# A delta-rule attention and a low-rank mixer in one kernel: two small products retiled, the square root table moved, a new order of all steps

## The chip, the cores and the metric

The kernel runs on one core of a Trainium2 chip. A core has five engines, each with its own in-order list of instructions: TensorE (PE, matmuls; its weight loads are listed as PEld), VectorE (DVE), ScalarE (ACT), GpSimd (POOL) and SyncE (SP, which here only issues DMA transfers). SP, POOL and ACT each own queues to the DMA engines. [...] TensorE reads its operands from SBUF and writes to PSUM, which holds 8 banks here, used as four pairs.

The metric is the device time of one execution in microseconds (us). A profile is one execution taken by the hardware profiler; it gives the span from the first to the last instruction and the execution's own time around it.

## What is computed

Two blocks follow one another (batch B=4, heads H=8, sequence S=768, head size D=48, model width 384, rank 32, hidden width 1536), all in fp32:

```python
# block 1: a delta-rule recurrence for each batch and head
k_n = k / (norm(k) + 1e-6)
for t in range(S):
    y[t]  = q[t] @ state
    v_old = k_n[t] @ state
    state = state + beta[t] * outer(k_n[t], v[t] - v_old)
# x: (B, S, 384), the heads side by side
# block 2: a mixer of low rank over the tokens, then a two-layer net over the channels
h = (x.transpose(0, 2, 1) @ U) @ V       # U: 768 x 32, V: 32 x 768
u = x + h.transpose(0, 2, 1)
out = u + relu(u @ w_ch1) @ w_ch2        # 384 -> 1536 -> 384
```

## The kernel before

**Units and chunks.** The recurrence is worked in chunks of 64 tokens. A unit n (0 to 7) is half a batch: 6 chunks of all 8 heads; batch b has the units 2b and 2b+1. For each unit there are, in this order: transfers of k, q, v and a shifted copy of k (`load`, line 524, issued by SP, POOL and, for unit 0, half of the keys by ACT); turning k and q to have the head size on the partitions (`turn`, TensorE transposes, line 639, in runs of six; the copy out of PSUM is `placed`, lines 648 to 653); products of the turned keys with keys and queries (`products`, line 666); the norms (`norms`, line 586: a square root on ScalarE, then VectorE from line 589); the inversion of a triangular matrix for each chunk and head. The inversion is a substitution on VectorE (`blocks`: transposed in at line 742, then the pairs of lines 751 and 757, transposed out at line 764), followed by small matmuls that join blocks (`joins`, lines 808, 822, 848 to 869, and copies by ScalarE, lines 813, 856, 875, 887). `prepare` (lines 971 and 982) makes from these the operands of the recurrence. VectorE does the substitutions of two units one after the other, since both use the same buffers.

**Recurrence.** `recur(b)` goes through the batch's 12 chunks, one after another. In each there is a product with the old state (line 1020), a subtraction on VectorE (line 1033), an update of the state (line 1048 on TensorE, 1059 on VectorE) and the outputs (lines 931 and 945, copied to X by ScalarE at line 915).

**Mixer.** `front(b, i)` handles 256 tokens (i = 0, 1, 2) of batch b. For i = 0 it first makes U^T x for the whole batch (line 1338), with PSUM's 128 partitions cut into four groups of 32, one for each column group of the array. Before the change, group g adds up the three blocks of 128 tokens with c = g mod 2: the groups 0 and 2 hold the sum over the even blocks, 1 and 3 the sum over the odd ones, each twice. VectorE copies it to `tt` (line 1344). V lies in `v_sb` four times below itself, so that 64 rows of V against 64 rows of `tt` add the two partial sums. The product with V (line 1357) is made of four matmuls, each on its own 64x64 quarter of the array: two halves of the output rows for each of two blocks of 128 tokens; VectorE adds it to X (line 1362), TensorE turns the sum (line 1381), ScalarE copies it to `ut` (line 1384).

**Channel net.** `wide(b, i)` does the first layer (`channels`, line 1442, relu at line 1407) and the second (`narrow`, line 1562) with a scheme that needs seven block products in place of eight; for the last batch the first layer too has such a scheme (`quick`, line 1241). Sums into X are at line 1482, the stores at lines 1488 and 1494.

**Weights.** U, V, w_ch1 and w_ch2 (slices 0 to 13) come as 64-bit numbers and are converted to fp32: a transfer (`start`, line 1131), a scaling on ScalarE (`raised`, line 1143), three steps on VectorE (lines 1157, 1164, 1171). Their three landing buffers are used in turn.

**Modes of the array.** A matmul whose operands use all 128 rows and columns takes the whole array. Smaller ones are put on tiles of it: 64x64 (lines 555, 666, 808, 822, 931 to 1048, 1357), 32x32 (848 to 869) or 128x32 (1338).

**What sets the order.** Every step is a `yield` of a Python generator. A text in the kernel (`ORDER`, lines 144 to 344) gives for each generator the positions of its steps in one list of 2139; `run` works it off in that order. An engine's list is its share of these steps in order. The costs given to `op(...)` and the conditions given to `need(...)` and `emitted(...)` served the search of that list; they put no wait into the program. The waits come from the data alone.

**Square root.** [...] The table with the square root is loaded by an instruction that the compiler puts ahead of the first operation that needs it. The kernel has an operation meant to bring that about early (line 535, a square root of one column `warm`), which in the order before stands at position 750, after the first norms.

Of the kernel before, what the change touches and what calls it, by code (L numbers as in the profile page):

```python
# [8 lines left out]
FP32 = mybir.dt.float32  # L9
# [7 lines left out]
L = 64  # L17
# [10 lines left out]
def kernel(  # L28
# [69 lines left out]
    def act(n):  # L98
        return 0.16 + n / 1200.0
# [45 lines left out]
    add_up b0 i0 f00: 658 659 660; add_up b0 i0 f03: 623 625 647; add_up b0 i1 f00: 774 778 789; add_up b0 i1 f03:  # L145
    794 808 809; add_up b0 i2 f00: 902 910 928; add_up b0 i2 f03: 978 981 985; add_up b1 i0 f00: 1073 1111 1134;
    add_up b1 i0 f03: 1122 1125 1132; add_up b1 i1 f00: 1253 1269 1279; add_up b1 i1 f03: 1276 1278 1292; add_up b1
    i2 f00: 1417 1426 1442; add_up b1 i2 f03: 1475 1481 1485; add_up b2 i0 f00: 1583 1621 1630; add_up b2 i0 f03:
    1643 1645 1653; add_up b2 i1 f00: 1724 1726 1731; add_up b2 i1 f03: 1797 1799 1801; add_up b2 i2 f00: 1872 1886
    1915; add_up b2 i2 f03: 1924 1925 1932; add_up b3 i0 f00: 2051 2052 2053; add_up b3 i0 f03: 2067 2068 2070;  # L150
    add_up b3 i1 f00: 2089 2090 2091; add_up b3 i1 f03: 2095 2096 2097; add_up b3 i2 f00: 2111 2112 2113; add_up b3
    i2 f03: 2105 2108 2109; blocks n0: 49 75 79 80 81 82 83 84 85 86 88 94 98 99 110 111 117 120; blocks n1: 126 142
    148 155 169 180 184 187 189 191 200 209 211 213 219 224 225 229; blocks n2: 478 498 502 503 506 511 514 517 518
    520 525 533 534 539 540 541 547 550; blocks n3: 686 699 708 710 719 720 725 727 733 736 738 740 743 744 747 748
    751 754 760 761 762 763 764 772 781 784 785 806 811 823 824 825 827 831; blocks n4: 947 959 970 971 979 986 987
    990 994 996 997 1000 1001 1016 1024 1029 1030 1033 1037 1043 1046 1047 1048 1051 1052 1053 1056 1057 1058 1062
    1065 1069 1071 1079; blocks n5: 1102 1139 1141 1143 1144 1153 1161 1163 1169 1176 1177 1178 1179 1190 1201 1209
    1211 1213 1215 1219 1221 1224 1227 1229 1235 1240 1248 1249 1252 1254 1257 1259 1262 1264; blocks n6: 1429 1451
    1452 1453 1457 1464 1471 1478 1490 1496 1499 1505 1507 1510 1514 1516 1526 1528 1535 1536 1537 1545 1546 1547
    1552 1553 1556 1558 1560 1562 1563 1565 1568 1573; blocks n7: 1595 1609 1614 1618 1632 1635 1648 1658 1661 1662  # L160
    1670 1674 1676 1681 1684 1687 1691 1693 1699 1700 1705 1711 1712 1714 1715 1718 1719 1722 1725 1729 1733 1738
    1739 1762; both f0: 2034; both f1: 2000; both f2: 1992; both f3: 2063; both f4: 1986; both f5: 2047; channels b0
    i0 e0: 522 524; channels b0 i0 e1: 535 546; channels b0 i0 e2: 549 558; channels b0 i0 e3: 561 581; channels b0
    i0 e4: 583 603; channels b0 i0 e5: 606 609; channels b0 i1 e0: 753 755; channels b0 i1 e1: 757 758; channels b0
    i1 e2: 765 766; channels b0 i1 e3: 767 769; channels b0 i1 e4: 770 771; channels b0 i1 e5: 777 786; channels b0
    i2 e0: 861 872; channels b0 i2 e1: 876 887; channels b0 i2 e2: 891 899; channels b0 i2 e3: 904 918; channels b0
    i2 e4: 925 940; channels b0 i2 e5: 942 968; channels b1 i0 e0: 1049 1059; channels b1 i0 e1: 1060 1064; channels
    b1 i0 e2: 1066 1067; channels b1 i0 e3: 1074 1080; channels b1 i0 e4: 1082 1084; channels b1 i0 e5: 1085 1108;
    channels b1 i1 e0: 1214 1217; channels b1 i1 e1: 1228 1230; channels b1 i1 e2: 1231 1232; channels b1 i1 e3: 1241
    1266; channels b1 i1 e4: 1267 1270; channels b1 i1 e5: 1272 1273; channels b1 i2 e0: 1369 1377; channels b1 i2  # L170
    e1: 1385 1387; channels b1 i2 e2: 1394 1408; channels b1 i2 e3: 1410 1427; channels b1 i2 e4: 1435 1444; channels
    b1 i2 e5: 1450 1469; channels b2 i0 e0: 1548 1569; channels b2 i0 e1: 1570 1577; channels b2 i0 e2: 1578 1579;
    channels b2 i0 e3: 1581 1594; channels b2 i0 e4: 1597 1600; channels b2 i0 e5: 1602 1603; channels b2 i1 e0: 1695
    1696; channels b2 i1 e1: 1698 1704; channels b2 i1 e2: 1710 1713; channels b2 i1 e3: 1728 1734; channels b2 i1
    e4: 1743 1744; channels b2 i1 e5: 1754 1785; channels b2 i2 e0: 1843 1846; channels b2 i2 e1: 1855 1856; channels
    b2 i2 e2: 1857 1861; channels b2 i2 e3: 1871 1883; channels b2 i2 e4: 1895 1902; channels b2 i2 e5: 1910 1921;
    copies f0: 2014 2018; copies f1: 1964 1987; copies f2: 1969 1974; copies f3: 2038 2040; copies f4: 1968 1971;
    copies f5: 2016 2036; cut f0 k0 to0: 2030; cut f0 k0 to1: 2035; cut f0 k1 to1: 2069; cut f1 k0 to0: 1990; cut f1
    k0 to1: 2079; cut f1 k1 to1: 2002; cut f2 k0 to0: 2050; cut f2 k0 to1: 2006; cut f2 k1 to1: 2004; cut f3 k0 to0:
    2049; cut f3 k0 to1: 2077; cut f3 k1 to1: 2062; cut f4 k0 to0: 2059; cut f4 k0 to1: 2007; cut f4 k1 to1: 2026;  # L180
    cut f5 k0 to0: 2056; cut f5 k0 to1: 2093; cut f5 k1 to1: 2057; diagonals n0 h0: 192 202 204 208 218 221;
    diagonals n0 h1: 164 178 183 188 198 207; diagonals n1 h0: 305 306 312 313 319 337; diagonals n1 h1: 262 265 276
    280 334 340; diagonals n2 h0: 585 592 594 613 637 648; diagonals n2 h1: 608 610 611 614 620 621; diagonals n3 h0:
    836 839 844 848 867 880; diagonals n3 h1: 843 845 879 886 888 890; diagonals n4 h0: 1088 1091 1092 1103 1124
    1136; diagonals n4 h1: 1093 1106 1107 1116 1130 1148; diagonals n5 h0: 1274 1280 1290 1315 1332 1337; diagonals
    n5 h1: 1308 1314 1340 1345 1348 1370; diagonals n6 h0: 1607 1626 1627 1629 1631 1636; diagonals n6 h1: 1587 1588
    1589 1601 1616 1617; diagonals n7 h0: 1765 1766 1767 1768 1812 1813; diagonals n7 h1: 1769 1773 1780 1787 1818
    1839; first f0: 2029; first f1: 1989; first f2: 1979; first f3: 2048; first f4: 2015; first f5: 2031; front b0
    i0: 485 501 504 508 510 512; front b0 i1: 523 532 548 551; front b0 i2: 644 653 654 664; front b1 i0: 1003 1013
    1023 1025 1036 1041; front b1 i1: 1075 1094 1152 1157; front b1 i2: 1301 1324 1334 1342; front b2 i0: 1506 1512  # L190
    1515 1529 1532 1533; front b2 i1: 1561 1574 1598 1610; front b2 i2: 1659 1660 1666 1669; front b3 i0: 1919 1920
    1926 1927 1931 1933; front b3 i1: 1936 1940 1945 1948; front b3 i2: 1949 1950 1954 1955; gather b0 i0 h0 c0
    finalFalse: 650; gather b0 i0 h0 c0 finalTrue: 638; gather b0 i0 h0 c1 finalTrue: 730 1181; gather b0 i0 h1 c0
    finalFalse: 693; gather b0 i0 h1 c0 finalTrue: 711 737; gather b0 i0 h1 c1 finalFalse: 695; gather b0 i0 h1 c1
    finalTrue: 716; gather b0 i1 h0 c0 finalFalse: 807; gather b0 i1 h0 c0 finalTrue: 814; gather b0 i1 h0 c1
    finalTrue: 856 1244; gather b0 i1 h1 c0 finalFalse: 819; gather b0 i1 h1 c0 finalTrue: 858 1220; gather b0 i1 h1
    c1 finalFalse: 829; gather b0 i1 h1 c1 finalTrue: 846; gather b0 i2 h0 c0 finalFalse: 973; gather b0 i2 h0 c0
    finalTrue: 983; gather b0 i2 h0 c1 finalTrue: 1045 1097; gather b0 i2 h1 c0 finalFalse: 998; gather b0 i2 h1 c0
    finalTrue: 1050 1192; gather b0 i2 h1 c1 finalFalse: 999; gather b0 i2 h1 c1 finalTrue: 1027; gather b1 i0 h0 c0
    finalFalse: 1126; gather b1 i0 h0 c0 finalTrue: 1147; gather b1 i0 h0 c1 finalTrue: 1204 1305; gather b1 i0 h1 c0  # L200
    finalFalse: 1166; gather b1 i0 h1 c0 finalTrue: 1202 1304; gather b1 i0 h1 c1 finalFalse: 1175; gather b1 i0 h1
    c1 finalTrue: 1182; gather b1 i1 h0 c0 finalFalse: 1283; gather b1 i1 h0 c0 finalTrue: 1296; gather b1 i1 h0 c1
# [140 lines left out]
    1841 1922 1929 1938 1941 1944 1951  # L343
    """
    ORDER = [x.rsplit(":", 1) for x in " ".join(ORDER.split()).split("; ")]
    ORDER = {int(y): name for name, at in ORDER for y in at.split()}

    def name_of(part):

# [1291 lines left out]
```

## Time and profile before

| | us |
|---|---|
| median of three runs | 614.36 |
| the three runs | 611.83, 614.36, 616.7 |
| the profiled execution, its own time | 617.97 |
| its span | 616.3 |
| TensorE busy in the span | 581.1 |
| VectorE busy | 393.1 |
| ScalarE busy | 232.4 |
| POOL busy | 96.5 |
| U^T x, line 1338, 96 records | 8.8 busy, 0.498 each |
| V product, line 1357, 96 records | 10.8 busy, 0.523 each |
| the one load of the square root table, at line 586 | 1.283 |

Times on the page are measured from the span's start. The time of one instruction is from its issue to its end; matmuls overlap, so a matmul's time is longer than its share of the engine, and the share is read from the distance of two starts. An fp32 matmul appears as two records. The row PEclk on the page is the clock granted to TensorE, in tenths of full speed, for each of 40 equal slices of the span. The chain of waits follows the last instruction back to what released it, step by step; a time on it is a time that the end had to wait for.

### The profile page before, as it was taken

How to read it: one execution, taken by the hardware profiler on the slowest of the kernel's cores; microseconds unless marked ns; L12 is line 12 of the kernel's file. 1: busy time of each engine (PE TensorE's matmuls, PEld its weight loads, DVE VectorE, ACT ScalarE, POOL GpSimd, SP SyncE). 2: the span in 40 equal slices, each digit the busy share in tenths (PEclk: the TensorE clock that was granted, in tenths of full speed). 3: DMA queues.
4: the chain of work that ended last, by engine and by line, in shares of the span. 5: the costliest groups of instructions: out<-in, count | busy, mean ns of one | idle time of the engine just before them, and what ended most of it. 6: DMA issues, size and time to landing. Idle time of an engine off the chain costs nothing.

```text
span 616.3 us, 23450 instructions
## 1 busy us (share of the span) xinstructions
PE 581.1 (94%) x10548; PEld 499.2 (81%) x10548; DVE 393.1 (64%) x971; ACT 232.4 (38%) x463; POOL 96.5 (16%) x169
## 2 busy tenths in 40 slices
PE   5598986899999999999999999999999999999997
PEld 4487875678888988888988988888989877655997
DVE  5878684688689616989697248998774124224352
ACT  2655754436512354126423452255152331234100
POOL 7141130401202501203101403013001000000000
PEclk9955555789999999999999999999999999999999
DMA  9924369512011510300122302211010000100010
GB/s 145 180 52 115 106 191 188 111 30 71 22 30 29 83 34 17 70 26 23 30 87 46 69 3 65 57 24 33 14 45 12 29 4 1 38 0 1 1 50 29
DMA packets 63845, 33.28 MB, mean 54 GB/s; under 512 B 50816, under 2 KB 61824, under 8 KB 63744
## 3 DMA queue, kind: packets, MB, share of 16 engines
q1 hardware_dynamic: 56800, 23.21, 17.0%
q0 software_dynamic: 5344, 8.27, 6.1%
q8 instruction: 83, 1.36, 0.9%
q10 hardware_dynamic: 1600, 0.30, 0.3%
q14 instruction: 18, 0.15, 0.1%
HBM read 27.03 MB, written 4.72 MB: 52 GB/s over the span
## 4 chain that ended last, share of the span: by engine, by line
PE 84%; DVE 7%; DMA 3%; ACT 2%; issue 2%; POOL 1%; SPq 0%; DVEq 0%; ACTq 0%; POOLq 0%
PE P L1562 28%; PE P L1442 22%; PE P L1241 7%; PE P L666 3%; PE P L639 3%; DMA wide<-in_moe_w_ch_dram 2%; PE P L1020 2%; PE P L971 2%; DVE xt L757 2%; PE P L982 2%; DVE prod L751 2%; PE P L945 2%; PE P L808 2%; PE P L1048 2%; PE P L822 2%
## 5 line engine op out<-in xcount | busy, mean ns | idle before, releaser
L1442 PE MATMUL P<-ut,w_sb 128*128 128x256 f32 x648 | 153.4, 387 | 0.9 <-ACT ut L1384 0.9
L1442 PEld LDWEIGHTS P<-ut,w_sb 128*128 128x128 f32 x648 | 119.5, 191 | 19.8 <-issue 2.2
L1562 PE MATMUL P<-w_sb,hs 128*128 128x192 f32 x540 | 96.0, 331 | 0.0
L1562 PEld LDWEIGHTS P<-w_sb,hs 128*128 128x128 f32 x540 | 87.2, 190 | 4.2 <-DVE prod L751 0.6
L757 DVE TENSOR_TENSOR xt<-xt,prod 128x112 f32<-128x112 f32 (+21 forms) x200 | 64.6, 323 | 6.9
L751 DVE TENSOR_TENSOR prod<-gs,xt 128x112 f32<-128x112 f32 (+21 forms) x200 | 63.8, 319 | 3.9
L1482 DVE TENSOR_TENSOR X<-X,P 128x192 f32<-128x192 f32 x84 | 28.9, 349 | 58.1 <-PE P L1562 57.9
L1407 ACT ACTIVATE hs<-P 128x512 f32<-128x512 f32 x54 | 32.1, 596 | 82.1 <-PE P L1442 77.2
L915 ACT COPY X<-P 64x192 f32<-64x192 f32 x96 | 30.0, 313 | 61.8 <-PE P L945 59.4
L1562 PE MATMUL P<-w_sb,S 128*128 128x192 f32 x288 | 50.8, 330 | 0.0
L1562 PEld LDWEIGHTS P<-w_sb,S 128*128 128x128 f32 x288 | 46.6, 190 | 2.2 <-issue 1.2
L524 POOL DMA_DIRECT2D slot<-in_k_dram x44 | 28.9, 664 | 114.4 <-PE P L1048 113.8
L639 PE MATMUL P<-ident,slot 128*128 128x128 f32 x192 | 31.6, 316 | 10.2 <-DMA slot<-in_k_dram 7.7
L666 PE MATMUL P<-slot 48*64 48x64 f32 x1536 | 33.7, 241 | 6.1 <-ACT slot L653 4.9
L1033 DVE TENSOR_TENSOR z<-slot,P 128x192 f32<-128x192 f32 x44 | 15.4, 351 | 36.5 <-PE P L1020 36.1
L666 PEld LDWEIGHTS P<-slot 48*64 48x64 f32 x1536 | 30.1, 153 | 10.5 <-ACT slot L653 7.3
L887 ACT COPY slot<-zz 32x384 f32<-32x384 f32 x64 | 32.4, 508 | 13.6 <-DVE zz L764 11.6
L639 PEld LDWEIGHTS P<-ident,slot 128*128 128x128 f32 x192 | 26.5, 164 | 12.5 <-issue 7.3
L653 ACT COPY slot<-P 128x768 f32<-128x768 f32 x30 | 23.4, 801 | 34.8 <-PE P L639 34.8
L1241 PE MATMUL P<-slot,w_sb 128*128 128x384 f32 x96 | 33.1, 486 | 0.0
L524 POOL DMA_DIRECT2D slot<-in_v_dram x32 | 20.8, 661 | 69.6 <-PE P L639 69.5
L1562 PE MATMUL P<-w_sb,slot 128*128 128x192 f32 x180 | 30.4, 327 | 0.9 <-DVE X L1482 0.9
(147 smaller groups left out, 881.7 us busy)
## 6 DMA issues: line engine op xcount, KB each, us to landing
out_dram<-X SPq DMA_DIRECT2D x22, 192.0 KB, 2.8
X<-in_moe_w_ch_dram SPq DMA_DIRECT2D x10, 384.0 KB, 4.3
wide<-in_moe_w_ch_dram SPq DMA_DIRECT2D x10, 384.0 KB, 5.0
slot<-in_k_dram SPq DMA_DIRECT2D x48, 72.0 KB, 3.8
slot<-in_k_dram POOLq DMA_DIRECT2D x44, 72.0 KB, 3.3
slot<-in_q_dram SPq DMA_DIRECT2D x32, 72.0 KB, 4.1
slot<-in_q_dram POOLq DMA_DIRECT2D x32, 72.0 KB, 3.4
slot<-in_v_dram SPq DMA_DIRECT2D x32, 72.0 KB, 3.1
```

Source lines behind the costliest of these rows:

```text
L524: queue.dma_start(out=t[half(1 - g if name == "z" else g), :, to, 0:D], in_=src[b, 4 * g + s, hf * UC * L : (hf + 1) * UC * L, :].rearrang ...
L639: nc.tensor.transpose(p_t[:, c // 3, c % 3], t[:, c, 2 * j : 2 * j + 2].rearrange("p s d -> p (s d)"), ident,)
L666: nc.tensor.matmul(p_g[half(g ^ (par * i)), par, c], kq[rows, c, j, 0, half(g)], kq[rows, c, j, i, half(g)], start=True, stop=True,)
L751: nc.vector.tensor_tensor(out=prod, in0=gb[:, :, j : j + 1, j + 1 :].to_broadcast([128, split, m, w]), in1=xb[:, :, 0:m, j : j + 1].to_bro ...
L757: nc.vector.tensor_tensor(out=xb[:, :, 0:m, j + 1 :], in0=xb[:, :, 0:m, j + 1 :], in1=prod, op=ALU.subtract,)
L887: nc.scalar.copy(pg[quarter(i), :, at, :, a : a + BK], cut(zc, h)[quarter(i)].rearrange("p r (c j) t -> p r c j t", j=2),)
L915: nc.scalar.copy(x[half(c % 2), c // 2, 4 * D * g : 4 * D * (g + 1)].rearrange("p (j r d) -> p r j d", r=2, d=D), states(p_y)[half(g)],)
L1241: nc.tensor.matmul(to, w, t, start=start, stop=stop, skip_group_check=True)
L1407: nc.scalar.activation(hs[:, fs[0] : fs[1] + 1 : fs[1] - fs[0]], p_f, ACTF.Relu)
L1442: nc.tensor.matmul(p_f[:, x], w(x, t), ut[:, t], start=(t == 0), stop=(t == KT - 1))
L1482: nc.vector.tensor_tensor(out=to, in0=to, in1=p, op=ALU.add)
L1562: nc.tensor.matmul(to, of[0], of[1], start=of[2], stop=of[3], skip_group_check=True)
```

## The change

- U^T x: group g now adds up the blocks with c = g mod 4, so the four groups hold four different partial sums, and each block is used once: 6 matmuls in place of 12 for each batch.
- V product: the four partial sums and the four copies of V make one product over all 128 rows, so each block of 128 tokens takes one matmul on the whole array in place of two on 64x64 quarters: 2 matmuls in place of 4 for each `front`, 24 in place of 48 in all.
- The square root of `warm` stands at position 25 in place of 750, and its memset comes first on VectorE.
- The list of all steps is new.

```diff
-    nc.vector.memset(P[:, :, 0:256], 0.0)
+    warm = const.tile([128, 1], FP32, name="warm")
+    nc.vector.memset(warm, 1.0)
+    nc.vector.memset(P[:, :, 0:256], 0.0)
...
         if halves == (1,) and (n, name) == (0, "k"):
-            yield op("act", 1.6)
+            yield op("act", 1.5)
             nc.scalar.sqrt(warm, warm)
+            emitted(("warm", 0))
...
+            yield need(("warm", 0))
...
         if i == 0:
-            o = yield op("pe", 1.95, "T", take="pair", words=48)
+            o = yield op("pe", 0.98, "T", take="pair", words=24)
             p_t = one(o)[:, 0:DM]
-            for y in range(NB // 2):
-                for g in range(4):
-                    c = 2 * y + g % 2
-                    nc.tensor.matmul(
-                        p_t[R * g : R * g + R], u_sb[:, c], x[:, c],
-                        start=(y == 0), stop=(y == NB // 2 - 1),
-                    )
+            for c in range(NB):
+                g = c % 4
+                nc.tensor.matmul(
+                    p_t[R * g : R * g + R], u_sb[:, c], x[:, c], start=(c < 4), stop=(c + 4 >= NB),
+                )
...
-        o = yield op("pe", 0.70, "Q", take="pair", words=16, flow=0.64)
+        o = yield op("pe", 0.65, "F", take="pair", words=8, flow=0.64)
         p_h = pair(o)[:, :, 0:DM]
-        for q in range(2):
-            for m, c in enumerate(cs):
-                nc.tensor.matmul(
-                    p_h[half(q), m], v_sb[half(m), c * 128 + L * q :][:, 0:L], tt[half(m)],
-                    start=True, stop=True,
-                )
+        for m, c in enumerate(cs):
+            nc.tensor.matmul(
+                p_h[:, m], v_sb[:, c * 128 : c * 128 + 128], tt, start=True, stop=True
+            )
```

Of the list, the positions (before and after) of some steps near the start:

| step | before | after |
|---|---|---|
| turn unit 0, k, pairs 0 and 1 | 6, 12 | 12, 32 |
| turn unit 1, k, pairs 0 and 1 | 61, 68 | 16, 33 |
| turn unit 0, q, pair 0 | 52 | 21 |
| turn unit 1, q, pair 0 | 123 | 42 |
| products of unit 0's keys, first step, pairs 0 and 1 | 16, 24 | 50, 46 |
| products of unit 1's keys, first step, pair 0 | 65 | 24 |
| load of the betas, first step | 14 | 39 |
| square root of `warm` | 750 | 25 |
| scaling of weight slice 11 | 441 | 509 |
| copies of unit 2's turned keys | 445, 446 | 447, 453 |
| first step of the first wide layer | 522 | 519 |

The planner's costs and conditions at a few other places change too, and the function that picks a step's form keeps picking the first one; neither puts an instruction into the program or takes one out.

## The prediction

> **What bounds the kernel now.** I read the page first, then the table of stages, the chain of waits, and the timeline of TensorE around the two products that change.
>
> ```profile
> span 616.3 us, 23450 instructions
> ...
> PE 581.1 (94%) x10548; PEld 499.2 (81%) x10548; DVE 393.1 (64%) x971; ACT 232.4 (38%) x463; POOL 96.5 (16%) x169
> ...
> PEclk9955555789999999999999999999999999999999
> ...
> PE 84%; DVE 7%; DMA 3%; ACT 2%; issue 2%; POOL 1%; SPq 0%; DVEq 0%; ACTq 0%; POOLq 0%
> ```
>
> TensorE is busy 94% of the span and makes 84% of the chain that ended last. The clock row shows a slow stretch near the start, so I cut the span at the first matmul of the wide layer (123.4 us) and at the first one of the last batch's shortened scheme (528.0 us). Columns of the table: stretch, length, busy time (instructions) of PE, PEld, DVE, ACT and POOL, granted clock, DMA share, GB/s.
>
> ```profile
> 0.00:31.30 31.30, 16.22 (x330) 14.06 (x330) 21.93 (x74) 15.25 (x27) 14.88 (x31) 0.95 0.97 160
> 31.30:62.80 31.50, 28.61 (x818) 27.09 (x820) 25.01 (x64) 18.63 (x36) 8.08 (x13) 0.55 0.32 82
> 62.80:99.80 37.00, 30.86 (x1052) 28.17 (x1051) 26.51 (x47) 20.82 (x44) 8.89 (x15) 0.55 0.63 160
> 99.80:123.40 23.60, 18.82 (x415) 15.17 (x415) 13.61 (x34) 10.80 (x20) 7.42 (x12) 0.64 0.67 139
> 123.40:528.00 404.60, 402.52 (x7559) 349.05 (x7560) 276.34 (x691) 148.44 (x295) 57.26 (x98) 1.00 0.16 37
> ```
>
> From 123.4 us on TensorE is idle for 2 us in 405: there the time is the sum of its matmuls, and any other engine's work is free. Before that it is idle for 29 of 123 us and runs at about half clock for 90 of them: there the end of the stage is set by DMA (first 31 us), by VectorE's substitution of one unit after the other, and by the serial recurrence of the first batch. So the change has two sums: TensorE work in the long stage, and the date of the first wide matmul. The set of instructions ahead of that matmul is the same in both orders but for the two products, so each us of that date is a us of the end.
>
> **U^T x and the V product.**
>
> ```profile
> 507.63 2.14 PE L1338 MATMUL P<-X,u_sb 128*32 128x384 f32 x24
> 509.70 1.56 PE L1442 MATMUL P<-ut,w_sb 128*128 128x256 f32 x6
> 511.19 0.88 PE L1357 MATMUL P<-tt,v_sb 64*64 64x384 f32 x8
> 512.01 2.22 PE L1562 MATMUL P<-w_sb,hs 128*128 128x192 f32 x12
> 514.07 0.87 PE L1381 MATMUL P<-ident,X 128*128 128x128 f32 x6
> ```
>
> Every fp32 matmul is two records. A full-array record of 384 columns takes 42.57/132 = 0.3225 us (the 132 records of line 1241 in the chain). U^T x: 24 records on four 32-column groups take 509.70 - 507.63 = 2.07 us, that is six rounds of four records (6 x 0.3225 = 1.94) and 0.13. Afterwards 6 matmuls, 12 records, fall on groups 0,1,2,3,0,1: four rounds, since groups 0 and 1 have two matmuls each. So 2.07 - 2 x 0.32 = 1.43, a gain of 0.64, not of half; x4 batches = **-2.6 us**. Bounds: 1.04 each (full halving, -4.1) and nothing.
>
> V: 8 records on four 64x64 quadrants take 512.01 - 511.19 = 0.82. Afterwards 4 full records in a row: 4 x 0.3225 = 1.29. Half the instructions, but each now uses the array alone: +0.47, x12 = **+5.7 us**. Bounds: against the bare two rounds (0.645) it is +7.7; if each V also spares a return to the full array (next term) it is +3.2.
>
> Returns to the full array: a run of 6 at line 1442 takes 1.30 us inside full-array work and 1.49 after another tiling; 12 records of line 1562 take 1.95 and 2.15. So a visit to another tiling costs 0.2. I counted runs of one tiling along TensorE's instruction list: between first wide matmul and shortened scheme 76 visits before (61 to 64x64, 12 to 32x32, 3 to 128x32), 68 after; ahead of it 7 and 8. Minus 7 x 0.2 = **-1.4 us** (0 to -2). Together **+1.7 us**, all but a few tenths in the saturated stage, where nothing hides it.
>
> **The square root table.**
>
> ```profile
> 6.62 6.45 DMA X<-in_beta_dram
> ...
> 16.28 1.28 ACT L586
> 17.57 0.27 ACT norm L586
> ```
>
> The load stands in the chain just ahead of the first norm, on which VectorE's substitution waits: taking it away gains **-1.28** there. It isn't gone: ScalarE still has two loads, and the second now follows its first copy, in front of the copy of the first turned keys (line 648); it is hidden there as long as that copy's readers, the first products of unit 0, come late anyhow, which the new order makes sure of. [...]
>
> **The new order at the start.** (1) In the old order the products of unit 0 (line 666) stand behind two runs of six transposes and start at 9.87. In the new list they stand behind seven such runs and 24 products of unit 1. The last of these runs reads a piece of unit 1's q that POOL issues as its 8th transfer: 3.74 + 7 x 0.66 = 8.4, and in the first 16 us POOL's q pieces land 6.8 us after issue: 15.2, and the run itself takes 1.4 at half clock (2.82 for 12): start at 16.6, **+6.7**. With the 4.4 of POOL's k pieces over the first 130 us it would be +4.3; both ends stay. Moved with them, and covered by this: SP issues unit 0's keys as transfers 1, 4, 8 and 9 (they were 1 to 4), the last at 0.82 + 8 x 0.65 = 6.0, landing 5.5 later at 11.5; POOL issues the betas as 9th and 11th (were 2nd and 5th), the last at 10.3, landing 6.0 later at 16.3, while the products run to 19.4; U's conversion on VectorE leaves an idle place for the substitution (counted next). Without that cover the betas would cost up to 3.2, against 13.07 before. Less 1.3 for the table: norm 5.4 late; VectorE has 0.6 more of other work inside that substitution (conversion of U, mask products: 2.45 against 1.84 us by their rows). So the substitution ends some 6.0 after 31.25. (2) What was done early is missing later: between it and the first prepare (31.39 to 54.14) TensorE no longer has one run of products (1.56) and one of transposes (1.54), nor most of the waits between (about 2): **-5**. But VectorE's second substitution follows the first, 26 us of VectorE work by the rows (old: done at 59.8; new: 37.3 + 26 = 63.3), and the first recurrence step stands behind its joins: +3.2 at that step (old 62.83). (3) Late in the stage:
>
> ```profile
> 98.90 6.38 DMA wide<-in_moe_w_ch_dram
> ...
> 106.30 0.81 ACT slot L653
> ...
> 107.15 1.56 PE P L666 x48
> ...
> 110.41 0.39 PE P L1048 x15
> ...
> 123.39 1.02 PE P L1442 x2
> ```
>
> ScalarE's scaling of weight slice 11 (line 1143) waits for its transfer, and the copy of unit 2's turned keys is queued behind it; behind that copy stand TensorE's products, and behind these the last recurrence step. The new order puts slice 11 (position 441, now 509) behind that copy (445, now 447). From the step before (99.76) to the last (110.19) it was 10.4; with transposes 2 x 1.4, products 3.1, two groups of recurrence matmuls 0.8, the copy 0.8 and 0.2 for semaphores it is 7.7: **-2.7**. The nine steps between (37 us) keep their work in another mixture; I take 0, bounds -3 and +3. Sum of the start: +3.2 - 2.7 = **+0.5**.
>
> Sum: 1.7 + 0.5 = +2.2 us on a profiled execution of 617.97 (span 616.3 and 1.7 around it). That one lies 3.6 above the median of the three runs, which scatter over 4.9, so I carry the difference over to the median: 614.36 + 2.2 = **616.6 us**. A measurement here tells about 1% (6 us) from no change; this is less.
>
> **Rivals.**
> A, the order pays in full: the late products cost nothing because the joins' -5 comes through, and V costs only its lower end. -2.6 + 3.2 - 1.4 - 1.3 - 2.7 - 5 = -9.8: 604.6. For it: TensorE was the engine waited for in 31 to 63 us, 28.6 busy of 31.5. Against: VectorE has 25 of these 31.5, and its work does not shrink.
> B, slower: the delay of the first substitution goes through whole. Place: unit 0's products behind the transposes of POOL's 8th transfer; price +6.0, in place of the start's +0.5; 614.36 + 1.7 + 6.0 = 622.1. It decides if those products start later than about 15 us and the late stall only shifts. For it: VectorE is a serial thread through both substitutions; against: the late wait on a weight slice swallows a shift, as that slice comes by itself.
> C, U^T x does not get shorter, because four different column groups with four different inputs do not run side by side (the old ones were pairs of equal inputs): 616.6 + 2.6 = 619.2.
> D, the clock falls in the long stage. In the stages up to 99.8 us it is 0.55 of full speed although TensorE is busy 83 to 91% of the time, so small tiles do not keep it up; a run of 6 at line 1442 took 2.73 us at 123.39 in place of 1.30. One such stretch of 15 us would cost 7.5: 624. Against it: no such stretch after 127 us in the old run, and fewer visits to small tiles now. [...]
>
> **Chances.** Forecast (616.6; by its own bounds 611 to 622) 0.47; A 0.17; B 0.22; C 0.06, within 1% too; D 0.08. Faster by over 1% 0.17, within 1% 0.53, slower 0.30. The range reaches down into A and up past D: 607 to 626.
>
> **What would show it.** Right: line 1357's successor at 4 records in 1.29 us and line 1338's at 12 in 1.4; the long stage about 2 us longer with TensorE still busy all through; first norm near 23 us, first recurrence step near 66, no wait of TensorE for the copy of unit 2's keys, first wide matmul at 123 to 125. Wrong: first wide matmul more than 5 us off, or waits of TensorE in the long stage above the present 2 us.

## The result, and the profile after

The changed kernel takes 625.11 us (median; 620.74 to 627.81) where the kernel before took 615.53 beside it: a ratio of 1.0153, with an interval of 1.0108 to 1.0199. It is slower by 1.5%. The forecast was 616.6, a change too small to be measured; the time lies inside its range (607 to 626), at the upper end.

The profiled execution took 627.81 us, 9.84 more than that of before. The page of after, its first part, its clock row, and the shares of the chain that ended last:

```profile
span 626.1 us, 23269 instructions
...
PE 587.2 (94%) x10452; PEld 508.0 (81%) x10452; DVE 393.2 (63%) x971; ACT 231.8 (37%) x463; POOL 96.3 (15%) x169
...
PEclk9655556798999999999999999999998999999999
...
PE 88%; DVE 4%; ACT 3%; issue 2%; DMA 1%; SPq 0%; DVEq 0%; ACTq 0%
```

TensorE has 96 fewer records and is busy 6 us longer, and the clock row has two 8s where before had only 9s once the long stage was under way. The table of stages of after, cut at the same events as before (end of the first substitution, first recurrence step, the step before the last, first wide matmul, first matmul of the shortened scheme; columns as before):

```profile
0.00:37.40 37.40, 19.93 (x384) 17.18 (x385) 22.35 (x74) 16.29 (x29) 18.69 (x38) 0.76 0.85 143
37.40:69.00 31.60, 27.72 (x784) 26.75 (x786) 25.91 (x65) 18.09 (x35) 4.16 (x7) 0.50 0.29 86
69.00:105.60 36.60, 30.47 (x1053) 28.26 (x1051) 24.69 (x46) 20.59 (x43) 8.92 (x15) 0.55 0.63 155
105.60:126.00 20.40, 17.23 (x392) 12.25 (x386) 13.70 (x33) 10.82 (x20) 7.34 (x12) 0.78 0.74 162
126.00:537.50 411.50, 407.42 (x7478) 357.81 (x7479) 277.21 (x693) 147.72 (x294) 57.17 (x98) 0.99 0.16 36
```

The first wide matmul comes at 126.0 in place of 123.4 (+2.6). The long stage takes 411.5 in place of 404.6 (+6.9; from first matmul to first matmul it is 404.4 before, and +7.0); TensorE is idle in it for 4.1 us in place of 2.1. The rest after it is the same within 0.3. So the question is what the 6.9 us are, since the two products were to bring 1.7 there.

The products themselves came out as worked out. The timeline of TensorE in after (start, length, line, operation, tiles, records):

```profile
515.20 1.48 PE L1344 MATMUL P<-X,u_sb 128*32 128x384 f32 x12
516.61 1.56 PE L1445 MATMUL P<-ut,w_sb 128*128 128x256 f32 x6
518.01 1.45 PE L1361 MATMUL P<-tt,v_sb 128*128 128x384 f32 x4
519.30 1.47 PE L1565 MATMUL P<-w_sb,hs 128*128 128x192 f32 x8
```

U^T x, 12 records, takes 516.61 - 515.20 = 1.41 (predicted 1.43); the V product, 4 records, 519.30 - 518.01 = 1.29 (predicted 1.29). What nobody asked for stands some 11 us into the long stage. The same view of after at 134 us; the last column is the idle time before a row and what ended it:

```profile
134.54 1.47 PE L645 MATMUL P<-ident,slot 128*128 128x128 f32 x12
136.30 1.19 PE L815 MATMUL P<-zz,slot 32*32 32x16 f32 x120 [0.29 <-ACT slot L660]
139.46 1.16 PE L815 MATMUL P<-zz,slot 32*32 32x16 f32 x72 [1.96 <-issue]
140.54 5.22 PE L1445 MATMUL P<-ut,w_sb 128*128 128x256 f32 x12
145.70 0.99 PE L829 MATMUL P<-zz 32*32 32x16 f32 x96
```

In the middle of one run of 192 small records (line 815, the joins of unit 2) TensorE stands still for 2 us, and "issue" says that it waited for nothing the profile shows. At 138.54, while it stands still, its clock falls from 1.0 to 0.5 on record, until 145.37, and the 12 records of line 1445 behind it take 5.16 us (145.70 - 140.54). The same run without a pause, in the kernel called "order only" below (the new order with the old products):

```profile
133.38 1.81 PE L815 MATMUL P<-zz,slot 32*32 32x16 f32 x192 [0.37 <-ACT slot L660]
135.12 2.86 PE L1449 MATMUL P<-ut,w_sb 128*128 128x256 f32 x12
137.91 1.11 PE L829 MATMUL P<-zz 32*32 32x16 f32 x96
```

There the 192 records take 1.74 us to the next start, in place of 4.24, and the 12 records 2.79. A smaller pause of the same kind (0.86 us between two starts) ends at 478.9, and a fall of 3.4 us begins at 479.9.

### The profile page after: what moved, and what is told of

Its sections match the earlier page's. It is cut to its first block, busy times and chain, and to the rows that moved or that the text cites. A ratio compares the mean times of both kernels' runs of the same rounds, so it can differ in the third digit from the quotient of the medians.

```text
span 626.1 us, 23269 instructions
## 1 busy us (share of the span) xinstructions
PE 587.2 (94%) x10452; PEld 508.0 (81%) x10452; DVE 393.2 (63%) x971; ACT 231.8 (37%) x463; POOL 96.3 (15%) x169
## 4 chain that ended last, share of the span: by engine, by line
PE 88%; DVE 4%; ACT 3%; issue 2%; DMA 1%; SPq 0%; DVEq 0%; ACTq 0%
PE P L1565 27%; PE P L1445 24%; PE P L1248 7%; PE P L645 4%; PE P L673 3%; PE P L1361 3%; PE P L1027 2%; PE P L978 2%; PE P L989 2%; PE P L952 2%; PE P L938 2%; PE P L815 2%; PE P L1055 2%; PE P L1384 1%; PE P L829 1%
## 5 line engine op out<-in xcount | busy, mean ns | idle before, releaser
L1445 PEld LDWEIGHTS P<-ut,w_sb 128*128 128x128 f32 x648 | 121.1, 193 | 18.7 <-ACT ut L1387 1.1
L1565 PEld LDWEIGHTS P<-w_sb,hs 128*128 128x128 f32 x540 | 88.9, 192 | 3.2 <-DVE prod L758 0.6
L673 PE MATMUL P<-slot 48*64 48x64 f32 x1536 | 31.7, 236 | 0.5 <-ACT slot L660 0.3
L1066 DVE TENSOR_TENSOR s<-s,P 128x192 f32<-128x192 f32 x40 | 14.0, 350 | 28.3 <-PE P L1055 28.3
L673 PEld LDWEIGHTS P<-slot 48*64 48x64 f32 x1536 | 28.4, 149 | 4.1 <-issue 1.9
```

The costliest lines, as they stand in the source:

```text
L673: nc.tensor.matmul(p_g[half(g ^ (par * i)), par, c], kq[rows, c, j, 0, half(g)], kq[rows, c, j, i, half(g)], start=True, stop=True,)
L1445: nc.tensor.matmul(p_f[:, x], w(x, t), ut[:, t], start=(t == 0), stop=(t == KT - 1))
L1565: nc.tensor.matmul(to, of[0], of[1], start=of[2], stop=of[3], skip_group_check=True)
```

## The experiments

**Which part of the change.** Four kernels on one chip, each with a part of the change.

The first has the old list of steps and only the two products new (6 matmuls for U^T x, 2 for each V product):

```diff
  ORDER = <the old list>
-            o = yield op("pe", 1.95, "T", take="pair", words=48)
+            o = yield op("pe", 0.98, "T", take="pair", words=24)
-        o = yield op("pe", 0.70, "Q", take="pair", words=16, flow=0.64)
+        o = yield op("pe", 0.65, "F", take="pair", words=8, flow=0.64)
```

> The kernel before with its own order of steps, and only the two products retiled. Theory (the new order is the main cause, the retiling costs what the prediction's sum said): U^T x -2.6 us, V +5.7, four visits to other tilings fewer (72 against 76 in the long stage) -0.8: +2.3 us, a ratio of 1.004; the first wide matmul stays at 123.4 +- 1 us, the long stage shows no fall of the granted clock, the runs of line 1357's successor have 4 records in 1.29 us. Rival R (the retiling is the main cause, by a clock that falls or by waits behind the full-array V product): +6 us or more, a ratio of 1.010 or above, with falls or more than 4 us of idle TensorE in the long stage.

The second has the new list and the old products (the same edit the other way round):

> The kernel after with its new order and early table, but U^T x and the V product as they were. Theory: what the two traces show beside the retiling stays: start +2.6 us, falls of the clock in the long stage +3.4, idle TensorE there +2.0, end +0.3, together +8.3 us, a ratio of 1.0135. Rival R (the retiling is the main cause): +3 us or less, 1.005 or below. Rival S (the falls of the clock come and go from run to run and have nothing to do with the order): the long stage without a fall, about +5 us, 1.008.

The third and the fourth splice the two lists, with the old products:

```diff
- ORDER = <the old list>
+ ORDER = <steps 0 to 518 of the new list>, then <the old list without them>      # new start
+ ORDER = <steps 0 to 521 of the old list>, then <the new list without them>      # new rest
```

> The first 519 steps of the new order (up to the first wide layer, with the early table), then the steps that are left in the old order; U^T x and V as before. Theory: first wide matmul at 126 us, +2.6; then the long stage as in the kernel before, so +2.6 us, a ratio of 1.004. If the falls of the clock in the long stage come from what the start leaves behind and not from the order of the steps after it, they show here too and it is +6, 1.010.

> The first 522 steps of the old order, then the steps that are left in the new order; U^T x and V as before (the square root of warm stands behind the first norms and loads nothing). Theory: first wide matmul at 123.4 us; a fall of the clock some 12 us behind it, behind the run of small matmuls and transposes of the third unit, as in the kernel after, and one near 480; with the idle times of the new order +5.5 us in the long stage, a ratio of 1.009. Rival S (the falls come and go with the run, or with the date at which the stage begins): no fall near these places, +2 us, 1.003.

| kernel | ratio to before (interval) | first wide matmul | long stage | pause of over 1.5 us in the long stage | fall of the clock with it (begin, length) |
|---|---|---|---|---|---|
| before | | 123.4 | 404.4 | none | none |
| products only | 1.0135 (1.0103 to 1.0168) | 122.4 | 409.7 | 2.1, to 139.4 | 140.6, 3.4 long |
| order only | 1.0099 (1.0066 to 1.0132) | 123.3 | 406.7 | 2.2, to 146.6 | 146.3, 3.4 long |
| new start | 1.0070 (1.0037 to 1.0103) | 125.0 | 403.5 | none | none |
| new rest | 1.0094 (1.0057 to 1.0131) | 121.4 | 407.4 | 2.6, to 144.4 | 144.9, 3.4 long |

My theory fell with the products: they were to cost 0.4% and cost 1.35%. The new order alone came below its 1.35% with 0.99%, and the two splices near theirs (0.4% and 0.9%). Products and order alone add up to 2.3%, and together they cost 1.5%. So there may be something that both lose, and lose once. The pause is in all three kernels that go through the long stage in another way, and not in the new start, whose 0.7% it can't explain. (A pause here is the distance of two starts. The falls begin 1.9 to 3.3 us after the last start ahead of the pause, in order only before the pause is over.) The waits of TensorE in the long stage, products only:

```profile
PE P L822 <- issue: 1.9, 1, 1.9
```

new rest:

```profile
PE P L1451 <- issue: 2.4, 1, 2.4
```

One stands in the joins, the other in front of a full-array matmul of the wide layer. Neither waits for data that the profile shows.

**What the pauses have in common.** The page's list of DMA queues has one named "instruction". In before and in after (packets, MB, share):

```profile
q8 instruction: 83, 1.36, 0.9%
```

```profile
q8 instruction: 82, 1.34, 0.9%
```

A packet is 16 KB. TensorE's list in before has 21,096 weight loads and matmul records and some 120 waits; divided by 83 that is 256 entries to a packet. (An fp32 matmul is four entries, two weight loads and two records: the 48 of line 1338 in before have 96 and 96. A transpose is two: the 192 of line 639 have 192 and 192.) So the list itself is brought in while the kernel runs. I counted the entries in the traces, in the order of their starts. In the fourteen profiles of this study there are nine pauses of 1.5 us and more in the long stage, and every one ends at an entry with the number 256 n - 63, n whole. Of the 396 distances of over 0.5 us between two starts behind 30 us, 74 end at such an entry, where chance would put one or two, and each of these 74 ends 0.9 to 1.8 us after a packet has landed (median 1.4). In after: the packet takes from 136.81 to 138.15, and TensorE goes on at 139.46. When the fetch begins TensorE is 139 entries into the packet that it has, and it stops at that packet's end: here one packet is worked off while one is fetched.

So: a run of small matmuls works off a packet in 1 to 2 us (line 815: 240 entries in the 1.02 us up to the pause), a packet needs 1.9 to 3.3 from the start of its transfer to its use (the 74), and whether TensorE pauses depends on where in such a run the packet ends. The retiled products take 24 and 8 entries out of the list ahead of that run; the new order changes what stands ahead of it. Both move the borders.

**Is it the count alone?** The kernel before, with eight tiny matmuls in front of U^T x of batch 0, overwritten at once:

```diff
             p_t = one(o)[:, 0:DM]
+            for c in range(8 if b == 0 else 0):
+                nc.tensor.matmul(
+                    p_t[R * (c % 4) : R * (c % 4) + R, 0:16], u_sb[:, c % 4], x[:, c % 4][:, 0:16], start=True, stop=True,
+                )
```

> The kernel before with 8 tiny matmuls (128 rows, 32 columns, 16 elements) in front of U^T x of batch 0, whose result is overwritten: 32 more entries in TensorE's instruction list, nothing else. Theory F (instruction packets): TensorE's list comes in packets of 256 entries over the queue named instruction; each waiting time of about 2 us that the profiles of the new variants show in the long stage ends 63 entries short of a multiple of 256, some 1.3 us after the packet landed, and a fall of the clock follows. Moving the packet borders by 32 entries puts, by the entries' times in the old trace, whole packets on stretches that TensorE works off in 1.3 us (at 145 us), 1.4 (at 418) and 2.3 (at 471), where before no such stretch is under 1.8: about two stalls of some 2 us and a fall of the clock behind one of them, +4 to +8 us, a ratio near 1.010, for matmuls that take 0.3 us. Rival S (the stalls come with the run or with transfers that happen to be under way) and rival R (they come from the retiled products): 1.001, no stall above 1.2 us in the long stage.

Measured: 1.0088 (1.0050 to 1.0125), +5.4 us for 0.3 us of work. The timeline of TensorE of this kernel:

```profile
142.05 0.48 PE L1446 MATMUL P<-ut,w_sb 128*128 128x256 f32 x1
144.56 3.29 PE L1446 MATMUL P<-ut,w_sb 128*128 128x256 f32 x14 [2.03 <-issue]
```

The pause comes where the expectation had put it (145 us), between two records of one run of the wide layer that wait for nothing. The ones at 418 and 471 did not come, and in this profile no fall of the clock follows. Its long stage is 405.1 us, 0.7 over that of before, so this one profile does not show where the 5.4 us of the times went. The products-only kernel once more, on the same chip:

> The old order with the retiled products, once more, as the companion of the run above on the same chip. Theory F: as before, a ratio near 1.0135, with the stall of 2 us near 139 us and a fall of the clock behind it. Rival S: the stall at another place or none, 1.005.

1.0106 (1.0066 to 1.0146), with the pause (1.6 us, to 136.8) and the fall (137.9) in their places again: it is not chance.

The same means, tried as a cure on the changed kernel, with 4 tiny matmuls (16 entries):

```diff
             p_t = one(o)[:, 0:DM]
+            for c in range(4 if b == 0 else 0):
+                nc.tensor.matmul(
+                    p_t[R * (c % 4) : R * (c % 4) + R, 0:16], u_sb[:, c % 4], x[:, c % 4][:, 0:16], start=True, stop=True,
+                )
```

> The kernel after with 4 tiny matmuls in front of U^T x of batch 0 (16 more entries in TensorE's list, the result is overwritten). Theory F: with the packet borders moved by 16 entries the stretch at 139 us, worked off in 2.4 us in the trace of after, is no whole packet any more, nor the one at 306 (1.9); the one at 478 (2.4) stays. So the stall of 2.0 us at 137.5 and the fall of the clock at 138.5 (6.8 us at half speed) go: -4 to -5 us, a ratio near 1.008 in place of 1.0153. Rivals S and R: 1.015, the stall still there.

1.0152 (1.0110 to 1.0195): nothing gained. The pause is still there, 2.3 us, 16 entries earlier in the run, to 138.9. I had counted the time of the whole packet; but the fetch began only at 136.18, some 0.5 us after the run had started behind a wait for a copy, so what counts is the run behind the wait. With 384 entries in one run no shift of 16 gets a border out of it. The other cure, breaking that run:

```diff
- turn, turn, joins, joins, joins, joins (96 small matmuls), channels e2, channels e3, ...
+ turn, joins, channels e2, turn, joins, channels e3, joins, joins, ...
```

> The kernel after with the steps of one stretch in another order: between the turns of unit 3 and the 96 small matmuls of unit 2's joins (line 815) come two half steps of the wide layer, so that no run of small matmuls is longer than 48 there. The number of entries ahead of the next batch is the same. Theory F: no packet is used up in less than 3 us there, no stall and no fall near 138 us: -4 to -5 us, a ratio near 1.008. A theory by which the clock falls because of the small tiles themselves and the wait only came beside it expects a fall there still, with some 2 us less: 1.012. Rival R: 1.015.

1.0189 (1.0148 to 1.0229): not better. The last two joins now stood next to the following 48 small matmuls of line 829, again 96 in a row, and the pause (2.5 us, to 141.2) and a fall (142.2) had moved there. It says nothing against the packets and nothing for the cure, and since a pause and a fall came together again, it does not tell the packets from small tiles as the cause of the fall.

**The decisive pair.** The kernel before with tiny matmuls at the head of TensorE's list, where it has nothing to do for 5 us; once 256 entries, so that every border falls where it was, and once 128:

```diff
+    for x in range(64):        # 32 in the other
+        r = slice(32 * (x % 4), 32 * (x % 4) + 32)
+        nc.tensor.matmul(
+            P[r, 0, 448:464], ident[r, r], ident[r, 32 * (x % 4) : 32 * (x % 4) + 16],
+            start=True, stop=True, skip_group_check=True,
+        )
     slots = [const.tile([128, 9792], FP32, name=f"slot{i}") for i in range(2)]
```

> The kernel before with 64 tiny matmuls (32x32, 16 elements, an unused corner of PSUM) at the head of TensorE's list, in the 5 us in which it has nothing to do: 256 more entries, one whole packet, so every border falls where it fell before. Theory F (where the packet borders fall decides the stalls): no stall of over 1.2 us in the long stage, the same time as before, a ratio of 1.000 (within 0.3%). Rival P (any added or removed entry costs, since it disturbs a tuned program, or the tiny matmuls cost by themselves): 1.006 or more.

> The same with 32 tiny matmuls: 128 entries, half a packet. Theory F: the borders move by half a packet, and by the entries' times in the old trace whole packets then fall on stretches worked off in 1.2 us (at 140 us, line 808) and 1.6 to 1.7 (near 300, 365, 430): stalls there, at least one of about 2 us, and +3 to +6 us, a ratio of 1.005 to 1.010. If the number of entries does not matter: 1.000, as with 256.

64 tiny matmuls: 1.0031 (0.9999 to 1.0063), not to be told from no change. 32 of them: 1.0170 (1.0125 to 1.0215), +10.4 us. Half the added work, and a loss as large as that of the whole change, larger than expected. The same steps in both, by the timeline of TensorE. With 256 entries:

```profile
140.32 0.77 PE L814 MATMUL P<-zz,slot 32*32 32x16 f32 x47
141.07 0.84 PE L645 MATMUL P<-ident,slot 128*128 128x128 f32 x6
141.75 2.75 PE L1448 MATMUL P<-ut,w_sb 128*128 128x256 f32 x12
```

With 128:

```profile
140.25 0.68 PE L814 MATMUL P<-zz,slot 32*32 32x16 f32 x36
145.11 0.39 PE L814 MATMUL P<-zz,slot 32*32 32x16 f32 x11 [4.18 <-issue]
145.44 1.54 PE L645 MATMUL P<-ident,slot 128*128 128x128 f32 x6
146.77 4.53 PE L1448 MATMUL P<-ut,w_sb 128*128 128x256 f32 x12
```

The run of 47 records is cut after 36 by a pause of over 4 us, at the place that the expectation named (140 us, line 808 of before), and the wide layer behind it takes 4.53 in place of 2.75, behind a fall of the clock (0.83 is granted from 142.60 to 144.00). Of the other places named one has a pause, of 1.2 us near 308. Why over 4 us: TensorE has used up its packet at 140.8, and the next fetch begins only at 142.60. In between the DMA engines are full (1.09 busy, 0.40 afterwards), as the stages of this profile show (the share of the DMA engines is the last figure but one):

```profile
140.70:142.60 1.90, 0.23 (x25) 0.13 (x13) 1.87 (x4) 0.00 (x0) 0.00 (x0) 1.00 1.09 336
142.60:144.00 1.40, 0.00 (x0) 0.00 (x0) 1.37 (x3) 0.00 (x0) 0.00 (x0) 0.83 0.40 74
```

The long stages of the two, 256 entries first:

```profile
124.00:527.50 403.50, 402.28 (x7559) 348.75 (x7559) 276.36 (x690) 148.26 (x295) 57.13 (x98) 1.00 0.17 37
```

```profile
125.50:537.10 411.60, 404.41 (x7558) 350.82 (x7559) 276.50 (x690) 148.28 (x295) 57.10 (x98) 0.99 0.16 35
```

8.1 us between two programs whose long stages are the same list of instructions; and where the pause is missing the clock stays up (1.00 over its long stage, 0.99 in the other), so it is the standstill that brings it down there and not the small tiles by themselves. This is shown: where the packet borders fall costs this kernel up to 8 us there (8.6 by the medians of the two, 615.87 and 624.43), and the kernel before has one of the good places.

**Breaking the run properly.** In the changed kernel, each half step of the wide layer between 126 and 155 us is put behind at most 48 small matmuls:

```diff
- turn, turn, joins x4 (96 small matmuls), channels e2, e3, joins x2 (48), channels e3, e4, ...
+ turn, joins, channels e2, turn, joins, channels e3, joins, channels e3, joins, channels e4, joins x2 (48), channels e4, ...
```

> The kernel after with steps moved inside one stretch (126 to 155 us): the half steps of the wide layer are put one by one between the runs of unit 2's joins, so that at most 48 small matmuls (192 entries) stand between two of them; the attempt before this one left 96 in one run behind it, and the stall moved there. Theory F: a packet then holds at least one half step of 1.3 us and takes 2.3 us or more: a stall of at most 0.9 us, no fall of the clock there: -3 to -5 us against after, a ratio of 1.006 to 1.010. If the fall comes from the small tiles and not from the stall, it shows somewhere in this stretch still: 1.015.

The timeline of TensorE of this kernel:

```profile
139.04 0.59 PE L824 MATMUL P<-zz,slot 32*32 32x16 f32 x48
140.50 1.56 PE L1454 MATMUL P<-ut,w_sb 128*128 128x256 f32 x6 [0.86 <-ACT hs L1419]
141.99 0.59 PE L824 MATMUL P<-zz,slot 32*32 32x16 f32 x48
142.51 1.56 PE L1454 MATMUL P<-ut,w_sb 128*128 128x256 f32 x6
144.00 0.59 PE L824 MATMUL P<-zz,slot 32*32 32x16 f32 x48
```

No pause named issue of over 0.7 us, no fall there. The fall went with the pause, though the small tiles stand less close there now as well. The time went from 1.0153 to 1.0126 (1.0080 to 1.0173), 1.7 us and within what the intervals leave open, where 3 to 5 were expected: in the long stage of its profile the groups of lines 815 and 1445 give 2.9 us back (a wait of 0.86 for a relu, above, is in this already), and those of lines 645, 829, 855 to 876 and 1565, with more changes of tiling among them, take 1.6 more. The second fall, at 478.5, is still there.

**The prediction's two gains at the start.** The kernel before, with two of the new order's pieces; TensorE's list is untouched:

```diff
- 750: load n0 namek halves(1,)  (the square root of warm)      441: raised i11
+  12: load n0 namek halves(1,)                                  447: raised i11, behind "placed n2"
+    nc.vector.memset(warm, 1.0)   first on VectorE
```

> The kernel before with two of the new order's pieces alone: the square root of warm at the 13th position (its memset first on VectorE), and ScalarE's scaling of weight slice 11 moved behind the copies of unit 2's turned keys. TensorE's list is the old one, entry for entry. By the prediction's terms: the first norm 1.3 us earlier; of the late stall 2.7 us gone; together -1.3 to -4.0 us at the first wide matmul, and as much at the end, a ratio of 0.994 to 0.998. Rival: the substitutions and the recurrence give the 1.3 back, or slice 11 itself comes later and is waited for: 1.000.

0.9989 (0.9957 to 1.0021): not to be told from no change. In its profile the gains are there: the first norm starts at 16.01 in place of 17.57, no copy of unit 2's keys is waited for, and the first wide matmul comes at 119.2, where the six other profiles with the old start, that of the 128 entries (125.5) left out, have 120.4 to 124.0 (mean 122.2). The times show -0.7 us (-2.6 to +1.3). What became of the rest was not followed up. No kernel of this study beats the one before.

## Why the prediction was wrong in its likeliest case

The change from before to after is 9.6 us where 2.2 were forecast, outside the forecast's own bounds (611 to 622). The range holds it only because it was stretched up past rival D, to which I gave 0.08 and which I put down to another mechanism; that is luck. Point by point, in the prediction's own terms.

- **U^T x, -0.64 each: right** (1.41 against the 1.43 forecast). Rival C falls: four different column groups do run side by side.
- **V, +0.47 each: right, a little low.** 1.29 behind full-array work, as worked out; behind another tiling 1.39, probably because V now pays the return itself. Over the eleven in the long stage 14.58 in place of 9.17: +0.49 each.
- **Returns to the full array, -1.4: about right.** In the products-only kernel, four visits fewer shorten line 1562 by 0.85.
- **Square root table and late stall: right in place, not worth their price at the end** (the last experiment).
- **The start, +0.5: mis-sized; +2.6 in the profiles.** The six kernels with the new start have their first wide matmul at 122.9 to 126.6 (mean 124.8), 2.6 above the old start's mean too. Step by step the forecast held where the trace gave a row: products of unit 0 at 15.6 (16.6 forecast), first joins at 37.42 (37.3), nine steps in 36.6 (37), the late step in 6.4 in place of 10.4 (7.7 forecast). The term that failed is "the first recurrence step stands behind its joins: +3.2": it came at 69.0, +6.1. The second substitution was not late: its last transpose (line 780) ended at 62.8, where 63.3 was forecast (59.8 before). What the forecast had too short is the time behind it. In both lists 96 small matmuls of the joins stand ahead of the step. Before:

```profile
59.27 1.49 PE L808 MATMUL P<-zz,hs 64*64 64x16 f32 x45
61.23 1.86 PE L822 MATMUL P<-zz,S 64*64 64x16 f32 x45 [0.46 <-ACT zz L813]
```

After:

```profile
63.75 5.00 PE L815 MATMUL P<-zz,hs 64*64 64x16 f32 x90
```

Two things came together. From the substitution's main transpose (lines 764 and 771, over at 58.7 and 61.6) to the first join it is 2.0 us in place of 0.5, behind other matmuls of TensorE and a pause of 0.7 named issue. And the joins run at half clock throughout (4.9 us, 63.60 to 68.50), where the record of before has full clock from 58.78 to 62.19; from the first join to the step it is 5.4 in place of 3.6. The prediction had no term for either. Of these 6.1 us the late stage gave 3.2 back: it takes 20.4 in place of 23.6.
- **Rival B** (the 6 us pass through whole) did come about up to the step before the last (105.6 in place of 99.8, +5.8), and its first condition held (products later than 15 us). Its second did not: the late stall went, and +2.6 was left.
  Pauses that end at a packet border stand ahead of the first wide matmul too: those of over 0.5 us from 30 us on add up to 4.0 in after and 2.1 in before. What they cost there was not tried.
- **Rival D** (the clock falls in the long stage) did, and I had given it 0.08. Its price, 7.5, is close to what the rows of after show for pauses and falls together: line 815's run 4.24 where the same run without a pause takes 1.74 (order only), +2.5; the 12 records of line 1445 +2.5; and around 479 us 16 records of line 952 in 1.31 in place of 0.34 and 12 of line 1565 in 3.60 in place of some 2, together +2.5. The profile of before has some of this too: 1.2 in its first run of line 1442, in a fall from 123.63 to 127.04 (2.66 to the next start, 1.49 in the profile of the last experiment), and perhaps a stop of 1.0 at 161.3, which ends at a packet border but is named a wait for a copy. So 5.3 to 6.3 of the difference are pauses and falls, by these rows. A run that takes them out alone is missing: the kernel with the run broken up has 2.9 of the first pause and its fall back in its profile, loses 1.6 to the mixing, and gained 1.7 in the times. But D's mechanism was wrong: I held small tiles to be the danger, and wrote against it "no such stretch after 127 us in the old run, and fewer visits to small tiles now". Not the number of visits mattered but one run of 384 entries, and where a packet ends in it. The page had shown the queue named "instruction" all along, and I read it as 0.9% of traffic.

The sum, profile against profile: start +2.6; the two products in the long stage 5.4 - 2.0 = +3.4; pauses and falls +5.3 to +6.3; the last stage +0.2; 9.84 was measured, so -1.7 to -2.7 is left for the returns to the full array (-1.4 forecast) and all else, by subtraction and not by a run of its own. Without the third item the forecast would have been some 1 to 2 us too low, by the 2.1 of the start.

What stays open: how far single runs are decided by this. The runs of one kernel scatter by 8 us, each kernel but the one with the products alone has one profile, and a pause of 2.5 us was once followed by no fall. How the 10.4 us of the 128 entries divide between the long stage (8.1 in the profiles) and the start was not tried either.

## What to carry to other kernels

Where an engine's list has long runs of very small instructions, read the page's instruction queue and look for pauses named "issue": an edit that only changes the number of instructions ahead of such a run can cost more than the edit saves (here 32 idle matmuls ahead cost 10.4 us). Try an edit in two or three versions that differ by some dozens of idle instructions before you believe its time. Breaking such a run took the pause and the fall away here, but changes of tiling ate much of the gain (1.6 of 2.9 us in the profile). And when parts of a change, measured alone, add up to more than the whole, look for something that each of them disturbs once.

## What the runs showed of the hardware

- TensorE's list arrives in packets of 256 entries (83 packets of 16 KB in before, for 21,096 records and some 120 waits), one ahead (in after, at 136.81, the next was fetched with TensorE 139 entries into the one it had); a packet took 0.9 to 1.7 us on its queue (the 74 pauses), and TensorE went on 0.9 to 1.8 us after it. While transfers of weights and keys were under way (DMA engines 1.09 busy), the fetch started late in the kernel with 128 entries: it began at 142.60, 3.3 us after TensorE had entered the packet ahead of it, and the pause was 4.35 us between two starts.
- Eight of the nine pauses over 1.5 us in the long stage had a fall of the clock within 2 us of their end, of 3.41 or 6.83 us; one of 2.5 us (before with 32 more entries) had none. A standstill of 1.6 us (products only, second profile) came with a fall, and near 478 us in three kernels with the new order 0.9 to 1.2 us, with small tiles ahead. In the eight cases the fall began 1.2 to 3.6 us after the last start ahead of the pause.
- In four profiles the record of the clock begins only at 56 to 60 us, and the page shows full clock ahead of it. The matmuls say otherwise: 48 records of line 808 near 40 us take 2.68 us in such a profile (new rest) and in that of before, where half clock is on record.
